# Layer 2 of a retention and two-layer feed-forward kernel: products of a folded pair accumulate in PSUM onto terms that ScalarE or VectorE wrote there, and a 256-token block keeps two tiles in a bank

## The chip, the cores and the metric

One core of a Trainium2 chip. The metric is device time in microseconds (us). A profile is one execution; engines are named as in it: PE (TensorE matmul), PEld (its weight loads), DVE (VectorE), ACT (ScalarE), POOL (GpSimd), SP (SyncE, which issues DMAs here).

## The reference

A retention (attention with a decay instead of a softmax) feeds two feed-forward layers over 2304 tokens:

```python
def _moe_ref(x, w_in, w_out):        # layer 1
    h = x @ w_in                     # 512 -> 2048
    g = np.maximum(0.01 * h, h)
    return g @ w_out                 # 2048 -> 512

def _moe2_ref(x, w_in, w_out):       # layer 2
    h = x @ w_in
    g = h - np.tanh(h)
    return g @ w_out

# reference: attn -> x (2304 x 512) -> layer 1 -> layer 2, all float32
```

## The kernel before

Every float32 operand of a feed-forward product is split into a high part (rounded) and a low part (the rest), and three matmuls stand for one: high x high, high x low, low x high.

The work of both layers is one list of steps. A step (m, g, t0, n, f) is one 128-wide tile of the hidden size in group g (four tiles, f = 0 to 3, are a group; there are four groups in a layer) for a block of n tokens from t0. The 2304 tokens are four blocks of 512 and one of 256. In layer 2 (m = 1) the block of 256 comes first in groups 0 to 2 and last in group 3. Let e be the first step of a layer-2 group: then e to e+3 are the 256-token steps and e+4 onward the 512-token steps.

What happens to a step s:

- `h_mm` or `h_folded` (PE) makes h, a 128 x n tile in one of three PSUM banks.
- `act_a` (ACT, then POOL): a square (L364), a tanh (L365), a second square (L372) and a Relu (L375), each reading what stands above it; POOL forms tanh times square (L368, called the cube below).
- `chain`: three DVE operations (h minus tanh, L387; a polynomial, L388; a predicated copy, L391), then ACT rounds the result into the high part of g (L393, the g copy) and POOL subtracts it for the low part (L394). The predicated copy is the last reader of the PSUM bank, which is then free.
- `o_mm` (PE): g times w_out, three steps later (`lag`), accumulated over a group in a second set of five banks: 12 matmuls of 512 columns for 512 tokens, 6 for 256 tokens; it can be issued in two halves (`part` 0 and 1).
- `evac` of the fourth step of a group moves or adds the sums to SBUF: in group 0 by copies that alternate between DVE (L497) and ACT (L495), later by DVE additions (L499).

In layer 2 a 512-token block is computed for two steps at a time (a *pair*, s and s+1): `h_folded` is a 2 x 2 block product with seven products in place of eight. Each product is 6 matmuls of 256 columns. It uses sums of weights (`ws`, prepared earlier) and differences of x (`xe`, made by `fold_x` between the last steps of layer 1 and the first pairs of layer 2: seven forms a block, each an ACT copy, L461, a POOL subtraction, L462, and for four of the seven a DVE subtraction, L459, ahead of them). The halves of the two banks p0 (for s) and p1 (for s+1) receive:

```python
        def first():
            product(a, left, of_x(0, 0), p1[:, left], start=True)
            product(sb, right, of_x(0, 1), p1[:, right])
            nc.scalar.activation(out=t_, in_=p1, func=AF.Copy)       # L318, 512 columns to SBUF
        def first_rest():
            product(a, right, of_x(1, 0), p0[:, left], start=True)
            product(sa, right, of_x(1, 1), p0[:, right], stop=True)
```

followed by four DVE additions of 256 columns (`add`, L303) that form the shared sums: p0 left, a sum in the tile mk, p0 right, and p1 right. The PE's order in a pair is: first (12 matmuls), half of the output product of step a = s-3, first_rest (12), its other half, second (6), half of step b = s-2, third (6), its other half, fourth (6).

The order of instructions on each engine is the order in which the Python code issues them, pair by pair and step by step (`layers`); each engine takes its own instructions in that order, with semaphores between engines. DMAs of weights and of stored xe tiles stand on SP's queue and are attached to steps (`splits`), as the forms of `fold_x` are.

Of the kernel before, what the change touches and what calls it, by code (L numbers as in the profile page):

```python
# [10 lines left out]
F32 = mybir.dt.float32  # L11
# [3 lines left out]
AF = mybir.ActivationFunctionType  # L15
ALU = mybir.AluOpType
PSUM = bass.MemoryType.PSUM

P = 128
# [4 lines left out]
LEAD = 16  # L24
# [11 lines left out]
def retention_moe_moe(  # L36
# [16 lines left out]
    nc = tc.nc  # L53
# [3 lines left out]
    KK = DM // P  # L57
# [5 lines left out]
    GF = 4  # L63
# [6 lines left out]
    pools = {}  # L70
# [56 lines left out]
    n_early = EARLY * GF  # L127

    def lag(s):
        return 2 if steps[s][0] == 0 else 3  # L130


    wide = w1i.dtype == I64
# [134 lines left out]
    def h_mm(s):  # L268
        m, g, t0, n, f = steps[s]
        w = wt[m, 0, g * GF + f]  # L270
        ps = pools["h"](s)
        for kk in range(KK):
            cs = slice(kk * P, (kk + 1) * P)
            for i, (wi, x) in enumerate(((0, xh), (0, xl), (1, xh))):
                nc.tensor.matmul(  # L275
                    out=ps[:, :n], lhsT=w[:, wi, cs], rhs=x[:, kk, t0:t0 + n],
                    start=kk == 0 and i == 0, stop=kk == KK - 1 and i == 2,
                )
        hp[s] = ps

    def h_folded(s):

        m, g, t0, n, f = steps[s]
        fg = g * GF + f
        a, b = wt[m, 0, fg], wt[m, 0, fg + 1]
        sa, sb = ws[fg][0], ws[fg][1]
        left, right = slice(0, HALF), slice(HALF, 2 * HALF)
        p0, p1 = pools["h"](s), pools["h"](s + 1)
        hp[s], hp[s + 1] = p0, p1

        def of_x(k, part):
            at = t0 + part * HALF
            return lambda i, kk: (xh, xl)[i][:, 2 * k + kk, at:at + HALF]

        def of_e(j):
            return lambda i, kk: xe[t0][:, j, i, kk, :]

        t_ = pools["t2"].tile([P, 512], F32, tag="t", name="t")
        mk = pools["t2"].tile([P, 512], F32, tag="mk", name="mk")
        early_tiles[s + 1] = t_, mk  # L300

        def add(out_, x, y):
            nc.vector.tensor_tensor(out=out_, in0=x, in1=y, op=ALU.add)  # L303

        def product(w, cols, x, out_, start=False, stop=False):
            for kk in range(2):
                at = cols.start + kk * P
                for j, (wi_, xi) in enumerate(((0, 0), (0, 1), (1, 0))):
                    nc.tensor.matmul(  # L309
                        out=out_, lhsT=w[:, wi_, at:at + P], rhs=x(xi, kk),  # L310
                        start=start and kk == 0 and j == 0, stop=stop and kk == 1 and j == 2,
                        skip_group_check=True,
                    )

        def first():
            product(a, left, of_x(0, 0), p1[:, left], start=True)
            product(sb, right, of_x(0, 1), p1[:, right])
            nc.scalar.activation(out=t_, in_=p1, func=AF.Copy)  # L318

        def first_rest():  # L320
            product(a, right, of_x(1, 0), p0[:, left], start=True)
            product(sa, right, of_x(1, 1), p0[:, right], stop=True)

        def first_sum():
            add(p0[:, left], p0[:, left], t_[:, left])

        def second():
            product(sa, left, of_e(0), p1[:, left])
            add(mk[:, left], p1[:, left], t_[:, right])

        def second_sum():
            add(p0[:, right], p0[:, right], mk[:, left])

        def third():
            product(sb, left, of_e(1), p1[:, left])
            add(p1[:, right], p1[:, left], t_[:, right])

        def fourth():
            product(b, right, of_e(2), p1[:, left], stop=True)

        return first, first_rest, first_sum, second, second_sum, third, fourth

    def g_at(s):
        m, g, t0, n, f = steps[s]
        at = LEAD if m == 0 and n < 512 else 0
        return slice(at, at + n)

    def act_a(s, tight=False):
        m, g, t0, n, f = steps[s]
        W, tp = pools["w"], pools["t"]  # L350
        h = hp[s][:, :n]
        if m == 0:
            gt = g_place(m)
            nc.scalar.activation(out=gt[:, 0, g_at(s)], in_=h, func=AF.Prelu, alpha=0.01)  # L354
            nc.scalar.activation(out=h, in_=h, func=AF.Prelu, alpha=0.01)
            tmp[s] = gt
            return
        u = tp.tile([P, W], F32, tag="u", name="u", bufs=3)
        v = u if tight else tp.tile([P, W], F32, tag="u", name="v", bufs=3)
        q = pools["t2"].tile([P, W], F32, tag="q", name="q", bufs=1)  # L360
# [14 lines left out]
        nc.scalar.activation(out=mk[:, :n], in_=u[:, :n], func=AF.Relu, bias=qb[:, 1:2])  # L375
        if tight:
            cube()
        tmp[s] = (v, t_, q, mk)

    def chain(s):  # L380
        m, g, t0, n, f = steps[s]
        h = hp.pop(s)[:, :n]
        if m == 0:
            v, gt = h, tmp.pop(s)
        else:
            v, t_, q, mk = (x[:, :n] for x in tmp.pop(s))
            nc.vector.tensor_tensor(out=h, in0=h, in1=t_, op=ALU.subtract)  # L387
            nc.vector.scalar_tensor_tensor(  # L388
                out=v, in0=q, scalar=RHO_A, in1=v, op0=ALU.add, op1=ALU.mult
            )  # L390
            nc.vector.copy_predicated(out=v, mask=mk.bitcast(U32), data=h)  # L391
            gt = g_place(m)
            nc.scalar.activation(out=gt[:, 0, g_at(s)], in_=v, func=AF.Copy)  # L393
        (nc.gpsimd if m else nc.vector).tensor_tensor(  # L394
            out=gt[:, 1, g_at(s)], in0=v, in1=gt[:, 0, g_at(s)].bitcast(F32), op=ALU.subtract
        )
        ga[s] = gt

    def o_mm(s, part=None):
        m, g, t0, n, f = steps[s]  # L400
# [11 lines left out]
        for d in {None: range(cnt), 0: range(cnt // 2), 1: range(cnt // 2, cnt)}[part]:  # L412
# [3 lines left out]
            for i, (wi, gi) in enumerate(((0, 0), (0, 1), (1, 0))):  # L416
                if m == 0:
                    l, r = w[:, wi, ds], gt[:, gi, g_at(s)]
                else:
                    l, r = gt[:, gi, ds], w[:, wi, :]  # L420

                nc.tensor.matmul(  # L422
                    out=o, lhsT=l, rhs=r,
                    start=f == 0 and i == 0 and d % pack == 0,
                    stop=f == GF - 1 and i == 2 and (d + 1) % pack == 0,
                    skip_group_check=pack > 1,
                )
# [450 lines left out]
    def layers():  # L878
        with ExitStack() as mc:
# [2 lines left out]
            cw_pool[0] = narrow.enter_context(  # L882
                tc.tile_pool(name="c1", bufs=2 * GF + 4, side="right")
            )
            ps_h = mc.enter_context(tc.tile_pool(name="ps_h1", bufs=3, space=PSUM))
            pools["h"] = lambda s: ps_h.tile([P, 512], F32, tag="h", name="h")
            pools["a"] = mc.enter_context(tc.tile_pool(name="ps_a1", bufs=5, space=PSUM))
            pools["w"] = 512

# [61 lines left out]
            e = per_group[1, 0][0]  # L951
            for t0, at in (
                (0, (-12, -11, -10, -9, -6, -6, -5)), (512, (-5, -5, -4, -4, -3, -3, -2)),
                (1024, (-2, -1, -1, 0, 4, 5, 6)), (1536, (7, 8, 9, 10, 12, 13, 14)),
            ):
                for i, op in zip(at, fold_x(t0)):
                    splits.setdefault(e + i, []).append(op)
# [23 lines left out]
            while s < end:  # L981
                m, g, t0, n, f = steps[s]
                if not folded(m, t0, n):
# [16 lines left out]
                first, first_rest, first_sum, second, second_sum, third, fourth = h_folded(s)  # L1000
                a, b = done[0], done[0] + 1
                assert (a, b) == (s - 3, s - 2)
                done[0] += 2
                first()
                o_mm(a, 0)
                first_rest()
                chain(s - 1)
                first_sum()
                cnt = steps[a][3] // P
                for d in range(cnt // 2):  # L1010
                    evac(a, d)
                o_mm(a, 1)
                evac(a, cnt // 2)
                second()
                second_sum()
                evac(a, cnt // 2 + 1)
                act_a(s)
                o_mm(b, 0)
                third()
                for op in splits.get(s, ()):  # L1020
                    op()
                o_mm(b, 1)
                fourth()
                act_a(s + 1)
                chain(s)
                assert steps[b][4] != GF - 1
# [79 lines left out]
```

## Time and profile before

| | us |
|---|---|
| median of 3 runs | 869.7 (869.04 to 871.87) |
| the profiled execution | 869.06, of it the span 867.1 |
| PE busy | 849.6 (98%) |
| DVE, ACT, POOL busy | 599.1 (69%), 452.0 (52%), 378.4 (44%) |
| layer 2 in the span | from about 474 to the end |

The page gives busy times over the whole span. Because PE is busy almost throughout, the views that matter are those by stretch: the chain of waits in order of time, which shows where it leaves PE, and the timelines of ACT, DVE and POOL around those places. A steady pair of layer 2 (24 matmuls of 512 columns and 42 of 256) follows the next without a gap.

### The profile page before, as it was taken

Reading aid. Unit: us, or ns where it says so; the run is one execution under the profiler, and the core shown is the slowest. Engines: PE = TensorE matmul, PEld = TensorE weight load, DVE = VectorE, ACT = ScalarE, POOL = GpSimd, SP = SyncE. Lnnn points to the kernel's source line nnn. Section 1 sums busy time; section 2 is a strip of 40 time slices with the busy share of each in tenths; the row PEclk is TensorE's granted clock in tenths of the full one; section 3 lists DMA queues with packets and bytes.
Section 4 is the critical chain, followed back from the end, with each engine's and each line's share of the span. In section 5 each row is a group of like instructions: output and inputs, shape, how many; then the busy total and the mean of one; then the engine's idle time right before and its main releaser. Section 6 shows DMA issues by size and latency. Waiting matters only on the chain.

```text
span 867.1 us, 15237 instructions
## 1 busy us (share of the span) xinstructions
PE 849.6 (98%) x5728; PEld 747.3 (86%) x5728; DVE 599.1 (69%) x1038; ACT 452.0 (52%) x899; POOL 378.4 (44%) x304
## 2 busy tenths in 40 slices
PE   6999999999999999999999999999999999999997
PEld 5889999888888888888888888888999899999996
DVE  5995777587786676658764677756666666666665
ACT  4553444453255334453544577666556566566663
POOL 2542222040036202464365587654555445545553
PEclk9999999999999999999999999999999999999999
DMA  9835663433464543644454512571225412563112
GB/s 341 315 122 173 219 208 122 146 121 113 134 211 189 179 121 99 243 170 136 181 184 156 195 73 74 222 285 73 78 96 183 159 73 74 207 231 122 49 50 74
DMA packets 38778, 134.43 MB, mean 155 GB/s; under 512 B 4400, under 2 KB 5936, under 8 KB 36656
## 3 DMA queue, kind: packets, MB, share of 16 engines
q1 hardware_dynamic: 38272, 133.25, 43.6%
q8 instruction: 45, 0.74, 0.3%
q10 hardware_dynamic: 432, 0.20, 0.1%
q14 instruction: 29, 0.24, 0.1%
HBM read 97.26 MB, written 36.18 MB: 154 GB/s over the span
## 4 chain that ended last, share of the span: by engine, by line
PE 90%; DVE 5%; issue 2%; POOL 2%; ACT 1%; DMA 0%; POOLq 0%; SPq 0%; DVEq 0%; ACTq 0%
PE a L422 39%; PE h L275 22%; PE h L309 17%; PE a L777 3%; PE x_b L752 3%; PE sc L626 2%; PE o L702 1%; PE o L691 1%; DVE cw L183 1%; DVE v L388 1%; PE x_c L659 1%; PE x_e L632 1%; POOL v L368 1%; DVE pt L640 1%; DMA qk<-in_kT 0%
## 5 line engine op out<-in xcount | busy, mean ns | idle before, releaser
L422 PE MATMUL a<-w 128*128 128x512 f32 (+1 forms) x1680 | 395.5, 377 | 1.2 <-ACT acc L495 0.6
L422 PEld LDWEIGHTS a<-w 128*128 128x128 f32 x1680 | 293.0, 188 | 49.9 <-POOL w L394 1.3
L256 POOL TENSOR_TENSOR w<-cw,w 128x512 fp32r<-128x512 f32 x80 | 112.7, 1427 | 234.1 <-ACT w L255 208.4
L275 PE MATMUL h<-xh,w 128*128 128x512 f32 (+1 forms) x672 | 187.1, 349 | 0.0
L368 POOL TENSOR_TENSOR v<-t,u 128x512 f32<-128x512 f32 (+1 forms) x76 | 93.8, 1234 | 113.7 <-ACT t L365 110.8
L275 PEld LDWEIGHTS h<-xh,w 128*128 128x128 f32 x672 | 119.5, 188 | 17.0
L354 ACT ACTIVATE w<-h 128x512 fp32r<-128x512 f32 (+1 forms) x68 | 37.2, 547 | 159.7 <-PE h L275 115.6
L394 POOL TENSOR_TENSOR w<-v,w 128x512 fp32r<-128x512 f32 (+1 forms) x76 | 97.1, 1277 | 47.8 <-ACT w L393 47.8
L275 PE MATMUL h<-xl,w 128*128 128x512 f32 (+1 forms) x336 | 117.0, 348 | 0.0
L309 PE MATMUL h<-xh,w 128*128 128x256 f32 x512 | 101.0, 281 | 0.4 <-DVE v L391 0.2
L364 ACT ACTIVATE u<-h 128x512 f32<-128x512 f32 (+1 forms) x80 | 44.3, 554 | 94.7 <-DVE h L303 67.6
L309 PEld LDWEIGHTS h<-xe,w 128*128 128x128 f32 x576 | 80.8, 189 | 10.6 <-DVE mk L303 2.6
L183 DVE SCALAR_TENSOR_TENSOR cw<-st,cw 128x512 uint32<-128x512 uint32 x96 | 86.5, 901 | 2.5
L388 DVE SCALAR_TENSOR_TENSOR v<-q,v 128x512 f32<-128x512 f32 (+1 forms) x76 | 55.7, 733 | 45.2 <-POOL v L368 45.0
L309 PEld LDWEIGHTS h<-xh,w 128*128 128x128 f32 x512 | 83.1, 190 | 3.3 <-DVE v L391 2.1
L309 PE MATMUL h<-xe,w 128*128 128x256 f32 x576 | 84.2, 282 | 1.2 <-DVE mk L303 1.2
L499 DVE TENSOR_TENSOR acc<-a,acc 128x512 f32<-128x512 f32 (+1 forms) x114 | 70.3, 656 | 16.2 <-PE a L422 16.2
L172 DVE TENSOR_SCALAR cw<-cw 128x512 f32<-128x512 f32 x64 | 33.9, 529 | 57.9 <-ACT cw L166 57.7
L309 PE MATMUL h<-xl,w 128*128 128x256 f32 x256 | 71.8, 281 | 0.0
L275 PEld LDWEIGHTS h<-xl,w 128*128 128x128 f32 x336 | 63.3, 188 | 8.6
L393 ACT ACTIVATE w<-v 128x512 fp32r<-128x512 f32 (+1 forms) x76 | 45.3, 596 | 46.9 <-DVE v L391 44.4
L387 DVE TENSOR_TENSOR h<-h,t 128x512 f32<-128x512 f32 (+1 forms) x80 | 51.4, 642 | 14.2 <-ACT t L365 13.2
(82 smaller groups left out, 1157.9 us busy)
## 6 DMA issues: line engine op xcount, KB each, us to landing
kept<-w SPq DMA_DIRECT2D x48, 512.0 KB, 3.4
w<-kept SPq DMA_DIRECT2D x48, 512.0 KB, 4.8
xe<-xkept SPq DMA_DIRECT2D x12, 1536.0 KB, 6.7
st<-in_w2i SPq DMA_DIRECT2D x16, 512.0 KB, 3.7
st<-in_w1i SPq DMA_DIRECT2D x12, 512.0 KB, 4.5
st<-in_w1o SPq DMA_DIRECT2D x12, 512.0 KB, 3.4
xkept<-xe SPq DMA_DIRECT2D x4, 1536.0 KB, 6.8
kv<-in_vn SPq DMA_DIRECT2D x16, 320.0 KB, 5.0
```

What stands on the lines that cost most here:

```text
L183: nc.vector.scalar_tensor_tensor(out=t["w"], in0=t[src], scalar=scalar, in1=t["w"], op0=op, op1=ALU.bitwise_or)
L256: nc.gpsimd.tensor_tensor(out=wp[:, 1, :], in0=wf, in1=wp[:, 0, :].bitcast(F32), op=ALU.subtract)
L275: nc.tensor.matmul(out=ps[:, :n], lhsT=w[:, wi, cs], rhs=x[:, kk, t0:t0 + n], start=kk == 0 and i == 0, stop=kk == KK - 1 and i == 2,)
L309: nc.tensor.matmul(out=out_, lhsT=w[:, wi_, at:at + P], rhs=x(xi, kk), start=start and kk == 0 and j == 0, stop=stop and kk == 1 and j == ...
L364: nc.scalar.activation(out=u[:, :n], in_=h, func=AF.Square)
L368: nc.gpsimd.tensor_tensor(out=v[:, :n], in0=t_[:, :n], in1=u[:, :n], op=ALU.mult)
L387: nc.vector.tensor_tensor(out=h, in0=h, in1=t_, op=ALU.subtract)
L388: nc.vector.scalar_tensor_tensor(out=v, in0=q, scalar=RHO_A, in1=v, op0=ALU.add, op1=ALU.mult)
L393: nc.scalar.activation(out=gt[:, 0, g_at(s)], in_=v, func=AF.Copy)
L394: (nc.gpsimd if m else nc.vector).tensor_tensor(out=gt[:, 1, g_at(s)], in0=v, in1=gt[:, 0, g_at(s)].bitcast(F32), op=ALU.subtract)
L422: nc.tensor.matmul(out=o, lhsT=l, rhs=r, start=f == 0 and i == 0 and d % pack == 0, stop=f == GF - 1 and i == 2 and (d + 1) % pack == 0, s ...
L499: nc.vector.tensor_tensor(out=dst, in0=a, in1=dst, op=ALU.add)
```

## The change

In a pair, ACT copies the left half of p1 into the left half of p0 (PSUM to PSUM), and the right half of p1 into t_ (SBUF), two copies of 256 columns for one of 512. The product that `first_rest` put into p0 with a start is now issued in `second`, without a start, on top of ACT's copy. The two sums that remain on DVE write p0 right and p1 right straight from p1 left and t_; the products `third_rest` and `fourth` come on top. PE's new order in a pair: first (12), half of a (6), second (12), the other half of a (6), third (6), third_rest (6), half of b (6), fourth (6), the other half of b (6). The number of matmuls is the same.

In the 256-token blocks of groups 0 to 2, two steps share a bank (`paired`): `act_a` and `chain` do nothing for the even step and run once, 512 columns wide, for the odd one. The output product of the first step of layer 2 is issued one step later (`lag` 4), inside the first pair. The PSUM banks of h are handed out from a list of free ones. The forms of `fold_x` for the two last blocks move: none is left in the first pair.

```diff
+    def paired(s):
+        return steps[s][0] == 1 and steps[s][3] == HALF and s < len(steps) - GF
+
+    h_free, h_bank = [0, 1, 2], {}
+
+    def h_tile(s, last=False):
+        h_bank[s] = h_free.pop(-1 if last else 0)
+        return pools["h"].tile([P, 512], F32, tag=f"h{h_bank[s]}", name="h")
...
-        p0, p1 = pools["h"](s), pools["h"](s + 1)
+        p0, p1 = h_tile(s, last=True), h_tile(s + 1)
...
         def first():
             product(a, left, of_x(0, 0), p1[:, left], start=True)
             product(sb, right, of_x(0, 1), p1[:, right])
-            nc.scalar.activation(out=t_, in_=p1, func=AF.Copy)
-
-        def first_rest():
-            product(a, right, of_x(1, 0), p0[:, left], start=True)
-            product(sa, right, of_x(1, 1), p0[:, right], stop=True)
-
-        def first_sum():
-            add(p0[:, left], p0[:, left], t_[:, left])
+            nc.scalar.activation(out=p0[:, left], in_=p1[:, left], func=AF.Copy)
+            nc.scalar.activation(out=t_[:, left], in_=p1[:, right], func=AF.Copy)
 
         def second():
+            product(a, right, of_x(1, 0), p0[:, left])
             product(sa, left, of_e(0), p1[:, left])
-            add(mk[:, left], p1[:, left], t_[:, right])
+
+        def add(out_):
+            nc.vector.tensor_tensor(out=out_, in0=p1[:, left], in1=t_[:, left], op=ALU.add)
 
         def second_sum():
-            add(p0[:, right], p0[:, right], mk[:, left])
+            add(p0[:, right])
 
         def third():
             product(sb, left, of_e(1), p1[:, left])
-            add(p1[:, right], p1[:, left], t_[:, right])
+            add(p1[:, right])
+
+        def third_rest():
+            product(sa, right, of_x(1, 1), p0[:, right], stop=True)
...
     def act_a(s, tight=False):
         m, g, t0, n, f = steps[s]
         W, tp = pools["w"], pools["t"]
+        if paired(s):
+            if f % 2 == 0:
+                return
+            n = 512
...
-                (1024, (-2, -1, -1, 0, 4, 5, 6)), (1536, (7, 8, 9, 10, 12, 13, 14)),
+                (1024, (-2, -2, -1, -1, 6, 7, 8)), (1536, (9, 9, 10, 11, 12, 13, 14)),
...
+                first()
+                while done[0] < s - 3:
+                    o_mm(done[0])
+                    evac(done[0])
+                    done[0] += 1
                 a, b = done[0], done[0] + 1
                 done[0] += 2
-                first()
                 o_mm(a, 0)
-                first_rest()
+                second()
                 chain(s - 1)
-                first_sum()
                 cnt = steps[a][3] // P
                 for d in range(cnt // 2):
                     evac(a, d)
+                second_sum()
                 o_mm(a, 1)
-                evac(a, cnt // 2)
-                second()
-                second_sum()
-                evac(a, cnt // 2 + 1)
+                third()
+                for d in range(cnt // 2, cnt):
+                    evac(a, d)
+                third_rest()
                 act_a(s)
                 o_mm(b, 0)
-                third()
                 for op in splits.get(s, ()):
                     op()
+                fourth()
                 o_mm(b, 1)
-                fourth()
                 act_a(s + 1)
                 chain(s)
```

## Rows read from the trace of the kernel before

**Rows 1.** Busy by stretch: start:end, length; PE, PEld, DVE, ACT, POOL; clock; DMA
```profile
500.00:510.00 10.00, 8.78 (x57) 7.65 (x55) 7.57 (x13) 7.66 (x14) 8.30 (x7) 1.00 0.15 61
...
486.57:569.30 82.73, 80.59 (x513) 71.53 (x512) 60.62 (x95) 57.35 (x105) 57.38 (x42) 1.00 0.31 121
569.30:664.00 94.70, 94.69 (x603) 85.50 (x602) 61.25 (x109) 58.05 (x110) 48.74 (x40) 1.00 0.36 134
664.00:841.77 177.77, 177.68 (x1131) 160.96 (x1130) 118.71 (x207) 107.22 (x196) 91.87 (x72) 1.00 0.35 128
841.77:867.10 25.33, 20.02 (x108) 16.41 (x107) 14.20 (x23) 10.59 (x26) 9.80 (x11) 0.97 0.18 63
```

**Rows 2.** Chain of waits in order of time, layer 2: start, length, engine, tile, line
```profile
486.57 1.41 PE h L309 x12
...
569.30 1.41 PE h L275 x12
...
664.00 1.41 PE h L275 x12
...
726.81 2.12 PE h L309 x18
728.93 1.36 PE a L422 x6
...
737.19 2.12 PE h L309 x18
...
841.77 1.41 PE h L275 x12
```

**Rows 3.** Waits of PE after 470: who for whom, total, times, longest
```profile
PE h L309 <- DVE mk L303: 1.2, 1, 1.2
```

**Rows 4.** Timeline of ACT: group 1's 256-token steps and first pairs, a steady pair
```profile
574.06 0.37 ACT L364 ACTIVATE u<-h 128x256 f32<-128x256 f32 x1
...
590.39 0.60 ACT L364 ACTIVATE u<-h 128x512 f32<-128x512 f32 x1 [3.50 <-DVE h L303]
...
594.92 0.61 ACT L393 ACTIVATE w<-v 128x512 fp32r<-128x512 f32 x1
595.44 0.58 ACT L318 ACTIVATE t<-h 128x512 f32<-128x512 f32 x1
...
727.60 0.60 ACT L364 ACTIVATE u<-h 128x512 f32<-128x512 f32 x1 [0.87 <-POOL v L368]
```

**Rows 5.** Timeline of PE: group 0's start, a late start, group 1, a steady pair
```profile
485.03 1.54 PE L422 MATMUL a<-w 128*128 128x512 f32 x6
...
502.69 0.97 PE L309 MATMUL h<-xe,w 128*128 128x256 f32 x6 [1.22 <-DVE mk L303]
...
594.48 0.38 PE L309 MATMUL h<-xh,w 128*128 128x256 f32 x1
...
726.64 0.87 PE L309 MATMUL h<-xe,w 128*128 128x256 f32 x6
```

**Rows 6.** Timeline of ACT in group 0: square to copy, with forms of fold_x between
```profile
503.22 0.60 ACT L364 ACTIVATE u<-h 128x512 f32<-128x512 f32 x1 [0.67 <-DVE h L303]
...
505.42 0.63 ACT L461 ACTIVATE xe<-acc 128x512 fp32r<-128x512 f32 x1
...
508.65 0.63 ACT L461 ACTIVATE xh<-acc 128x512 fp32r<-128x512 f32 x1
509.17 0.60 ACT L318 ACTIVATE t<-h 128x512 f32<-128x512 f32 x1
```

**Rows 7.** Timeline of DVE: step e+1 of group 0; a chain in group 1
```profile
483.01 0.42 DVE L387 TENSOR_TENSOR h<-h,t 128x256 f32<-128x256 f32 x1
...
595.14 0.69 DVE L388 SCALAR_TENSOR_TENSOR v<-q,v 128x512 f32<-128x512 f32 x1
595.94 0.74 DVE L391 COPY_PREDICATED v<-mk,h 128x512 f32<-128x512 uint32 x1
```

**Rows 8.** Timeline of POOL: the low part of g in group 1
```profile
595.61 1.38 POOL L394 TENSOR_TENSOR w<-v,w 128x512 fp32r<-128x512 f32 x1 [0.50 <-ACT w L393]
```

More of the change, by code (lines that the diff above doesn't have):

```diff
@@ L129, in lag @@
     def lag(s):
-        return 2 if steps[s][0] == 0 else 3
+        if steps[s][0] == 0:
+            return 2
+        return 4 if s == per_group[1, 0][0] else 3
+    def paired(s):
[4 more added lines that the diff above has]
+        return pools["h"].tile([P, 512], F32, tag=f"h{h_bank[s]}", name="h")
     wide = w1i.dtype == I64
@@ L270, in h_mm @@
         w = wt[m, 0, g * GF + f]
-        ps = pools["h"](s)
+        two = paired(s)
+        half = two and f % 2
+        ps = hp.pop(s - 1) if half else h_tile(s + two)
+        at = half * n
         for kk in range(KK):
@@ L275, in h_mm @@
                 nc.tensor.matmul(
-                    out=ps[:, :n], lhsT=w[:, wi, cs], rhs=x[:, kk, t0:t0 + n],
-                    start=kk == 0 and i == 0, stop=kk == KK - 1 and i == 2,
+                    out=ps[:, at:at + n], lhsT=w[:, wi, cs], rhs=x[:, kk, t0:t0 + n],
+                    start=not half and kk == 0 and i == 0,
+                    stop=(half or not two) and kk == KK - 1 and i == 2,
+                    skip_group_check=two,
                 )
@@ L298, in h_folded @@
         t_ = pools["t2"].tile([P, 512], F32, tag="t", name="t")
[L299 to L303, printed above, removed]
+        early_tiles[s + 1] = t_, pools["t2"].tile([P, 512], F32, tag="mk", name="mk")
         def product(w, cols, x, out_, start=False, stop=False):
@@ L317, in first, with g_cols @@
             product(sb, right, of_x(0, 1), p1[:, right])
-            nc.scalar.activation(out=t_, in_=p1, func=AF.Copy)
-        def first_rest():
-            product(a, right, of_x(1, 0), p0[:, left], start=True)
-            product(sa, right, of_x(1, 1), p0[:, right], stop=True)
-        def first_sum():
-            add(p0[:, left], p0[:, left], t_[:, left])
+            nc.scalar.activation(out=p0[:, left], in_=p1[:, left], func=AF.Copy)
+            nc.scalar.activation(out=t_[:, left], in_=p1[:, right], func=AF.Copy)
         def second():
+            product(a, right, of_x(1, 0), p0[:, left])
             product(sa, left, of_e(0), p1[:, left])
-            add(mk[:, left], p1[:, left], t_[:, right])
+        def add(out_):
+            nc.vector.tensor_tensor(out=out_, in0=p1[:, left], in1=t_[:, left], op=ALU.add)
         def second_sum():
-            add(p0[:, right], p0[:, right], mk[:, left])
+            add(p0[:, right])
         def third():
             product(sb, left, of_e(1), p1[:, left])
-            add(p1[:, right], p1[:, left], t_[:, right])
+            add(p1[:, right])
+        def third_rest():
+            product(sa, right, of_x(1, 1), p0[:, right], stop=True)
         def fourth():
             product(b, right, of_e(2), p1[:, left], stop=True)
-        return first, first_rest, first_sum, second, second_sum, third, fourth
+        return first, second, second_sum, third, third_rest, fourth
     def g_at(s):
         m, g, t0, n, f = steps[s]
-        at = LEAD if m == 0 and n < 512 else 0
+        at = LEAD if m == 0 and n < 512 else f % 2 * n if paired(s) else 0
         return slice(at, at + n)
+    def g_cols(s):
+        return slice(0, 512) if paired(s) else g_at(s)
     def act_a(s, tight=False):
@@ L381, in chain @@
         m, g, t0, n, f = steps[s]
+        if paired(s):
+            if f % 2 == 0:
+                return
+            n = 512
         h = hp.pop(s)[:, :n]
+        h_free.append(h_bank.pop(s))
         if m == 0:
@@ L392, in chain @@
             gt = g_place(m)
-            nc.scalar.activation(out=gt[:, 0, g_at(s)], in_=v, func=AF.Copy)
+            nc.scalar.activation(out=gt[:, 0, g_cols(s)], in_=v, func=AF.Copy)
         (nc.gpsimd if m else nc.vector).tensor_tensor(
-            out=gt[:, 1, g_at(s)], in0=v, in1=gt[:, 0, g_at(s)].bitcast(F32), op=ALU.subtract
+            out=gt[:, 1, g_cols(s)], in0=v, in1=gt[:, 0, g_cols(s)].bitcast(F32),
+            op=ALU.subtract,
         )
         ga[s] = gt
+        if paired(s):
+            ga[s - 1] = gt
     def o_mm(s, part=None):
@@ L419, in o_mm @@
                 else:
-                    l, r = gt[:, gi, ds], w[:, wi, :]
+                    c = g_at(s).start + d * P
+                    l, r = gt[:, gi, c:c + P], w[:, wi, :]
                 nc.tensor.matmul(
@@ L884, in layers @@
             )
-            ps_h = mc.enter_context(tc.tile_pool(name="ps_h1", bufs=3, space=PSUM))
-            pools["h"] = lambda s: ps_h.tile([P, 512], F32, tag="h", name="h")
+            ps_h = mc.enter_context(tc.tile_pool(name="ps_h1", bufs=1, space=PSUM))
+            pools["h"] = ps_h
             pools["a"] = mc.enter_context(tc.tile_pool(name="ps_a1", bufs=5, space=PSUM))
@@ L999, in layers @@
                     continue
-                first, first_rest, first_sum, second, second_sum, third, fourth = h_folded(s)
+                first, second, second_sum, third, third_rest, fourth = h_folded(s)
+                first()
[3 more added lines that the diff above has]
+                    done[0] += 1
                 a, b = done[0], done[0] + 1
```

## The prediction, made before the changed kernel was run

> **What bounds the kernel now.** I read the busy times by stretch first, then the chain of waits in order of time over layer 2, then the timelines of ACT, DVE and POOL at the places where the chain leaves PE.
>
> The stretches [rows 1] show PE busy for 177.68 of 177.77 us in groups 2 and 3, and 94.69 of 94.70 in group 1; DVE, ACT and POOL are busy for two thirds or less of these. The chain [rows 2] gives the price of a matmul in a full stream: 18 of 256 columns in 2.12 us, 0.1178 each, and six of 512 in 1.36, 0.2267 each. A pair has 42 and 24 of them, 10.38, and this is the distance of 726.81 from 737.19: a steady pair has nothing to give. What an edit can save is only what PE loses against this count:
> - group 0, 486.57 to 569.30: 82.73. It holds eight pairs (336 narrow matmuls, 39.6) and 174 wide ones (39.4): 79.0, lost 3.7.
> - group 1, to 664.00: 94.70. 384 narrow, 216 wide: 94.2, lost 0.5.
> - groups 2 and 3, to 841.77: 177.77. 720 narrow, 408 wide: 177.3, lost 0.5.
>
> So 4.7 us in all. The tail after 841.77 keeps its code (the last group's 256-token block is not paired). The losses lie where pairs follow a 256-token block, whose output products are half as long; the largest single wait is for a DVE sum into mk [rows 3], a sum that goes.
>
> **Part by part.** *Matmuls:* same number, same sizes: 0.
>
> *DVE sums, two of four gone:* in a steady pair DVE is not on the chain: 0. In group 0 and after 256-token blocks the waits for them go with the 4.7, which I count as returned in full; what comes in their place is priced next.
>
> *ACT's copy comes onto PE's path.* This decides. Before, ACT's copy into t_ (L318) was read by DVE only, and PE needed p1 left free for second, after 12 more matmuls and half an output product. Now second begins by accumulating onto the copy in p0, so PE stops after first and half of a until it has landed, and the rest of PE's queue (second, a's other half, third and on) stands behind it. On ACT the copy stands behind everything issued before it: four operations of act_a(s), four of act_a(s+1), the g copy of s. These start when third_rest of the pair ahead has ended. I compare two times from that end to second.
>
> PE's side, steady: half of b (1.36), fourth (0.71), other half of b (1.36), first (1.41), half of a (1.36): 6.20. In the second pair after a 256-token block, b and a are 256-token steps: three halves of 0.68, so 4.16.
>
> ACT's side: 0.25 from the end of the last slot to the square (fourth's six matmuls from 726.64 end their slots at 727.35 [rows 5], the square starts at 727.60 [rows 4]); square to copy with ACT never idle 5.05 (590.39 to 595.44 [rows 4], just this place in group 1); the copy; 0.10 to restart PE (six matmuls that had waited took 0.97, otherwise 0.87 [rows 5]). A 256-column copy from PSUM to PSUM is not in the trace: below, half of the copy of 512 columns, 0.29; above, that copy itself, 0.58; the nearest row, a 256-column square out of PSUM, is 0.37 [rows 4], and I take it. Sum 5.77. The Trainium skill ("ScalarE: Activation LUTs", section "What ACT_TABLE_LOAD costs") puts an ACTIVATE with immediate operands at 186 ns plus 0.833 ns a column, by estimate 0.40 here; by it the seven waits counted below would be 0.2 longer together.
>
> - Steady pairs: 6.20 against 5.77, room of 0.43: 0. A copy of 0.58 still fits.
> - Second pair after the block, groups 0, 1 and 2: 5.77 - 4.16 = 1.6 each, 4.8 in all. Before, first_rest was issued there at 594.48 [rows 5] while the copy began at 595.44 [rows 4], and nobody waited for it.
> - Pairs of group 0 with forms of fold_x. Each form puts an ACT copy into that run: 503.22 to 509.17 with two of them is 5.95 [rows 6], so 6.67 against 6.20, wait 0.5; a third adds 0.52 (508.65 to 509.17), wait 1.0; one alone fits. By the new positions the runs that end in the third, fifth and sixth pair have two, that of the fourth three: 3 x 0.5 + 1.0 = 2.5. In the three, the odd step's form waits besides for its DVE subtraction, which is queued behind the predicated copy: from 0 to about 1 us each, I take 0.2, so 0.6. Together 3.1; bounds 0 (if ACT catches up) and 5.5.
>
> *The 256-token block, two tiles a bank.* Fewer, wider operations (0.60 for 512 columns against 2 x 0.37 on ACT [rows 4]) on engines with room: 0 for groups 1 and 2. But the pair's g comes later than the first tile's alone did. In group 0 DVE starts this chain at 483.01, held by four evacuations [rows 7]; subtract (0.6 to the next), polynomial (0.8 to the next), predicated copy 0.74 [rows 7], g copy 0.61 [rows 4], POOL 1.38 [rows 8], with 0.05 to 0.1 between engines: low part ready at about 487.3. PE reaches the product of step e, moved behind first, at 485.03 + 1.41 = 486.44 [rows 5], and needs the low part at its second matmul, 486.67: wait 0.7 (0 to 1.0). In groups 1 and 2 this product has two steps more, no wait.
>
> *First and second pairs:* the copy and the first DVE sum are each covered by half a product of 0.68 only, and need about 0.7: 0.05 each time, 0.15 a group, 0.45 in all.
>
> *Banks:* first now writes the bank that was free longest, so it waits for no predicated copy; ACT's copy into the other comes later than that bank's last reader. 0 (the saving is in the 4.7). *Forms moved ahead of layer 2:* one step of layer 1 gets one more; PE has not lost there: 0, up to 0.5.
>
> Sum: 0.7 + 4.8 + 3.1 + 0.45 = 9.05 lost against 4.7 lost now: +4.3. The profiled execution took 869.06 (span 867.1 and about 2 around it): 873.4. The median shown is 0.64 above that execution, so 874.0 as a median.
>
> **Rivals.**
> 1. *Faster: DVE was the limit and ACT keeps time.* For it: PE's largest wait is for DVE. Place: second in the second pair of groups 0 to 2. It decides from where ACT's run from square to copy is under 3.4 us (4.16 less 0.25, 0.37 and 0.10). Then the waits for copies are gone in every pair, the 4.7 come back less 1.15 for the product of e and the short covers: 869.06 - 3.6 + 0.64 = 866.1. Against it: the 5.05 is the same nine operations at the same place, measured.
> 2. *No change: only the short second pairs wait.* If forms find room (ACT's run begins earlier, or DVE without two sums lets them through), losses are 0.7 + 4.8 + 0.45 = 5.95 against 4.7: 871.0. For it: two forms miss the cover by 0.5 only. Against it: DVE does not order these ACT copies.
> 3. *Steady pairs wait too.* The room of 0.43 goes where the copy is as long as one of 512 columns (0.2 more) and a predicated copy holds the g copy by 0.3 or more: 0.1 to 0.3 in each of some 20 pairs, 4 on top: 878.
> 4. *The clock falls.* PE now stands still 1.6 us at a time. The longest stand in the trace is 1.2 us, and the stretch around it has a granted clock of 1.00, the 2.4 GHz level [rows 1]; the tail, with more idling, 0.97. At 1.2 GHz the 10.38 of a pair could double, +10 after each of three such waits: 900. The Trainium skill ("TensorE: Matmul & The Clock Gate", section "HAM oscillation — how this bites in real kernels") warns of this level where PE idles between bursts; no run here yet shows it.
>
> That the change does not do what it says is not a case of its own: the code leaves no other order on ACT.
>
> **How the numbers follow.** A measurement of this kernel can tell about 0.3%, 2.6 us, from no change: same is 867.1 to 872.3. Forecast 0.66, own range 871 to 877 (forms from 0 to 5.5, the product of e from 0 to 1): of it 0.54 slower, 0.12 same. Rival 1, 0.10: 0.08 faster, 0.02 same (it could return half). Rival 2, 0.13: same. Rival 3, 0.09: slower. Rival 4, 0.02: slower. That gives faster 0.08, same 0.27, slower 0.65. Range 870.0 to 878.0: it leaves out rival 1, rival 4 and half of rival 3.
>
> **What would show it.** In the chain of waits, PE after half of a in the second pair of groups 0, 1 and 2 released by an ACT copy into h, idle 1.6 us; the same, 0.5 to 1.0 us, in the third to sixth pair of group 0; the second matmul of step e released by POOL's low part. No wait for a DVE sum over 0.2. Groups 1 and 2 each about 1.2 us longer than now, the pairs after their second 10.38 apart. The prediction is wrong if the ACT copies end before PE has issued half of a in these pairs, or if steady pairs are not 10.38.

## The result and the profile after

The changed kernel takes 874.49 us (median of 6 runs, 873.78 to 876.14), the kernel before 870.05 (6 runs, 869.04 to 871.87): a ratio of 1.0052, 95% interval 1.0037 to 1.0067. It is slower, by half a per cent; 874.0 was forecast. The profiled execution took 874.01, its span is 872.2.

First the page's busy times of the changed kernel, then its busy times by stretch (columns as in [rows 1]). The stretches begin at the first step of groups 0, 1 and 2 of layer 2 and at the last group's 256-token block:

```profile
PE 850.6 (98%) x5728; PEld 746.7 (86%) x5728; DVE 570.3 (65%) x956; ACT 451.7 (52%) x901; POOL 370.9 (43%) x292
```
```profile
473.99:571.53 97.54, 93.76 (x590) 82.40 (x590) 58.40 (x84) 62.50 (x119) 60.83 (x45) 1.00 0.37 137
571.53:667.69 96.16, 94.78 (x603) 85.34 (x602) 54.22 (x86) 58.03 (x108) 46.85 (x36) 1.00 0.36 132
667.69:846.99 179.30, 177.90 (x1130) 160.91 (x1130) 105.30 (x168) 107.73 (x202) 88.43 (x68) 1.00 0.35 126
846.99:872.20 25.21, 20.02 (x108) 16.41 (x107) 13.93 (x22) 9.44 (x24) 9.63 (x11) 0.94 0.18 63
```

DVE does 28.8 us less in all, and the kernel is longer. Groups 1, and 2 with 3, now take 96.16 and 179.30, before 94.70 and 177.77 [rows 1]: 1.5 more each. Group 0 takes 97.54; before it went from 474.05, the first row below, to 569.30 [rows 2], 95.25: 2.3 more. The tail is what it was. These make 5.3, and the spans differ by 5.1.

```profile
474.05 1.41 PE h L275 x12
```

What PE waited for in layer 2, first as the matmuls have it and then as the weight loads have it (total, times, longest):

```profile
PE h L321 <- DVE v L412: 4.2, 3, 1.4
PE h L321 <- ACT h L330: 1.7, 4, 0.8
PE a L450 <- POOL w L418: 0.9, 3, 0.4
PE h L321 <- DVE h L338: 0.3, 1, 0.3
```
```profile
PEld h L321 <- ACT h L330: 9.6, 11, 1.8
PEld h L321 <- DVE h L338: 2.9, 8, 0.7
```

L330 is the copy into p0, L338 a DVE sum, L418 the low part of g. The three longest waits stand under DVE's polynomial (L412), which PE does not read. The timelines around the second pair of group 1 show what happened, ACT first, then DVE, PE and PE's weight loads:

```profile
592.59 0.60 ACT L383 ACTIVATE u<-h 128x512 f32<-128x512 f32 x1 [2.38 <-PE h L321]
...
597.11 0.61 ACT L417 ACTIVATE w<-v 128x512 fp32r<-128x512 f32 x1
597.63 0.36 ACT L330 ACTIVATE h<-h 128x256 f32<-128x256 f32 x1
597.93 0.36 ACT L331 ACTIVATE t<-h 128x256 f32<-128x256 f32 x1
```
```profile
597.34 0.69 DVE L412 SCALAR_TENSOR_TENSOR v<-q,v 128x512 f32<-128x512 f32 x1
```
```profile
595.83 0.84 PE L450 MATMUL a<-w 128*128 128x512 f32 x3
598.04 0.38 PE L321 MATMUL h<-xh,w 128*128 128x256 f32 x1 [1.38 <-DVE v L412]
```
```profile
598.04 0.19 PEld L321 LDWEIGHTS h<-xh,w 128*128 128x128 f32 x1 [1.80 <-ACT h L330]
```

PE has issued half of a at 596.51 (595.83 and three of 0.2267) and starts second at 598.04: 1.53 later, 0.05 after ACT's copy ended. The polynomial ended at 598.03, 0.04 after the copy. The profile infers the releaser from semaphore events, and for the matmul it named the later of the two, for the weight load the copy; e2 below shows that it is the copy. ACT's run from square to copy is 5.04 (592.59 to 597.63), before 5.05 at this place [rows 4]: the same run, which PE did not have to await then.

A steady pair has room, as forecast. ACT's copy, PE's second and the second of the next pair, in group 3:

```profile
776.10 0.36 ACT L330 ACTIVATE h<-h 128x256 f32<-128x256 f32 x1
```
```profile
776.89 0.28 PE L321 MATMUL h<-xh,w 128*128 128x256 f32 x1
...
787.28 0.28 PE L321 MATMUL h<-xh,w 128*128 128x256 f32 x1
```

The copy ends 0.43 before PE would go on in any case, and the pairs there keep their distance of 10.38 (10.39 by these two rounded times).

### The profile page after: what moved, and what is told of

Its sections match the earlier page's. It is cut to its first block, busy times and chain, and to the rows that moved or that the text cites. A ratio compares the mean times of both kernels' runs of the same rounds, so it can differ in the third digit from the quotient of the medians.

```text
span 872.2 us, 15121 instructions
## 1 busy us (share of the span) xinstructions
PE 850.6 (98%) x5728; PEld 746.7 (86%) x5728; DVE 570.3 (65%) x956; ACT 451.7 (52%) x901; POOL 370.9 (43%) x292
## 4 chain that ended last, share of the span: by engine, by line
PE 87%; DVE 4%; ACT 3%; DMA 2%; POOL 2%; issue 2%; POOLq 0%; ACTq 0%; SPq 0%; DVEq 0%
PE a L450 38%; PE h L289 21%; PE h L321 17%; PE a L805 3%; PE x_b L780 3%; PE o L730 1%; PE sc L654 1%; PE o L719 1%; DVE cw L194 1%; DMA cm_sb<-in_cmask 1%; POOL v L387 1%; DMA acc<-in_w1i 1%; ACT q L391 1%; DVE pt L668 1%; DVE v L412 1%
## 5 line engine op out<-in xcount | busy, mean ns | idle before, releaser
L387 POOL TENSOR_TENSOR v<-t,u 128x512 f32<-128x512 f32 x70 | 92.2, 1317 | 130.2 <-ACT t L384 124.7
L289 PEld LDWEIGHTS h<-xh,w 128*128 128x128 f32 x672 | 119.5, 188 | 17.1
L321 PE MATMUL h<-xh,w 128*128 128x256 f32 x512 | 106.7, 282 | 5.9 <-DVE v L412 4.2
L418 POOL TENSOR_TENSOR w<-v,w 128x512 fp32r<-128x512 f32 x70 | 91.1, 1301 | 45.5 <-ACT w L417 45.5
L321 PEld LDWEIGHTS h<-xh,w 128*128 128x128 f32 x512 | 85.4, 190 | 11.6 <-ACT h L330 9.6
L527 DVE TENSOR_TENSOR acc<-a,acc 128x512 f32<-128x512 f32 (+1 forms) x114 | 70.7, 656 | 22.2 <-PE a L450 22.2
L321 PEld LDWEIGHTS h<-xe,w 128*128 128x128 f32 x576 | 78.4, 189 | 7.4 <-DVE h L338 2.9
L412 DVE SCALAR_TENSOR_TENSOR v<-q,v 128x512 f32<-128x512 f32 x70 | 53.8, 768 | 33.2 <-POOL v L387 31.5
L338 DVE TENSOR_TENSOR h<-h,t 128x256 f32<-128x256 f32 x64 | 27.7, 432 | 63.6 <-PE h L321 62.3
```

Source lines behind the costliest of these rows:

```text
L289: nc.tensor.matmul(out=ps[:, at:at + n], lhsT=w[:, wi, cs], rhs=x[:, kk, t0:t0 + n], start=not half and kk == 0 and i == 0, stop=(half or ...
L321: nc.tensor.matmul(out=out_, lhsT=w[:, wi_, at:at + P], rhs=x(xi, kk), start=start and kk == 0 and j == 0, stop=stop and kk == 1 and j == ...
L412: nc.vector.scalar_tensor_tensor(out=v, in0=q, scalar=RHO_A, in1=v, op0=ALU.add, op1=ALU.mult)
L418: (nc.gpsimd if m else nc.vector).tensor_tensor(out=gt[:, 1, g_cols(s)], in0=v, in1=gt[:, 0, g_cols(s)].bitcast(F32), op=ALU.subtract,)
L527: nc.vector.tensor_tensor(out=dst, in0=a, in1=dst, op=ALU.add)
```

## Experiments

Eleven variants were run beside the kernel before. The part of the span ahead of layer 2 differs by up to 2.4 us between profiles though its code hardly does, so I compare stretches of layer 2, from the first step of one group to that of the next, in us. The ratios hold that part as well: e2 is 3.2 us above the changed kernel by the ratios and 1.8 by the stretches.

| kernel | group 0 | group 1 | groups 2, 3 | ratio to before (95%) |
|---|---|---|---|---|
| before | 95.25 | 94.70 | 177.77 | |
| changed | 97.54 | 96.16 | 179.30 | 1.0052 (1.0037 to 1.0067) |
| e1_no_copy | 96.67 | 95.67 | 178.75 | 1.0036 (1.0023 to 1.0049) |
| e2_wide_copy | 98.51 | 96.56 | 179.76 | 1.0089 (1.0074 to 1.0104) |
| e3_block_only | 94.47 | 94.70 | 177.75 | 0.9988 (0.9979 to 0.9997) |
| e4_body_only | 99.28 | 96.17 | 179.24 | 1.0071 (1.0057 to 1.0085) |
| e5_dve_copy | 101.11 | 99.53 | 182.20 | 1.0168 (1.0149 to 1.0187) |
| e6_forms_only | 93.77 | 94.68 | 177.78 | 0.9984 (0.9975 to 0.9993) |
| e7_no_act | 96.53 | 95.60 | 178.74 | 1.0028 (1.0018 to 1.0039) |
| e8_evac_first | 93.78 | 94.67 | 177.80 | 0.9987 (0.9978 to 0.9996) |
| e9_no_act_no_sum | 92.64 | 94.61 | 177.70 | 0.9952 (0.9939 to 0.9966) |
| e10_evac_act | 92.30 | 94.66 | 177.78 | 0.9968 (0.9958 to 0.9979) |
| e11_no_sum | 96.62 | 95.88 | 178.93 | 1.0042 (1.0025 to 1.0058) |

**Is it ACT's copy? Take it away (e1), make it wider (e2).**

```diff
# e1
-            nc.scalar.activation(out=p0[:, left], in_=p1[:, left], func=AF.Copy)
-            product(a, right, of_x(1, 0), p0[:, left])
+            product(a, right, of_x(1, 0), p0[:, left], start=True)
# e2
-            nc.scalar.activation(out=p0[:, left], in_=p1[:, left], func=AF.Copy)
+            nc.scalar.activation(out=p0, in_=p1, func=AF.Copy)
```

> The changed kernel without ACT's copy of p1 left into p0 left; the term that the copy carries is left out of the result, and the product that came on top of it starts its bank itself. Theory (PE waits for this copy, which stands in ACT's queue behind nine operations of the pair ahead): the waits in the second pair of groups 0 to 2 (1.5 each) and in pairs three to six of group 0 (0.5, 1.0, 0.5, 0.5) go, with about 0.1 of restart each: 867 (0.997 of before). What is left in the second pairs is a wait for the predicated copy that frees p0's bank, 0.1 to 0.2. Rival (the wait in the second pairs is for DVE's polynomial, as the trace's releaser column has it, and ACT's copy only ends about then): those three waits stay, 871.

> The changed kernel with ACT's first copy of a pair made 512 columns wide (all of p1 into all of p0); the right half of p0 is written over by DVE's sum later. Theory: the copy takes about 0.58 instead of 0.36, so each of the seven waits for it grows by 0.22 and the run of one form (pair seven of group 0) begins to wait by 0.2: +1.7, 876.2 (1.007 of before); steady pairs, with room of 0.43, stay at 10.38. Rival (PE waits for something else that ends about then): 874.5, no change. Rival (steady pairs have no room): some 20 pairs by 0.2, +4 more, 880.

e2 did as the theory says: layer 2's three stretches grew by 1.8 against the changed kernel (1.7 expected), steady pairs did not, but for 0.2 in one of group 2. Its waits of PE name the copy in all places, seven of them, as many as had been counted:

```profile
PE h L321 <- ACT h L330: 7.4, 7, 1.6
```

With the copy's end moved by 0.2, the polynomial no longer coincides with it. But e1 missed: 1.9 came back of 5.3, not some 7. PE's waits in e1:

```profile
PE h L321 <- DVE h L337: 1.5, 4, 0.8
PE h L321 <- ACT t L330: 1.0, 3, 0.3
```

L330 is here ACT's other copy, which reads p1 right; PE waits for it before it writes p1 left. L337 is DVE's first sum. So the copy into p0 does hold PE, but something stands right behind it.

**What stands behind it (e7, e9, e11).** e7 leaves out both copies, e11 the first DVE sum, e9 all three.

```diff
# e7, against e1
-            nc.scalar.activation(out=t_[:, left], in_=p1[:, right], func=AF.Copy)
-            nc.vector.tensor_tensor(out=out_, in0=p1[:, left], in1=t_[:, left], op=ALU.add)
+            nc.vector.tensor_tensor(out=out_, in0=p1[:, left], in1=xl[:, 0, :HALF].bitcast(F32), op=ALU.add)
# e9, against e7
         def second_sum():
-            add(p0[:, right])
+            pass
# e11, against the changed kernel
         def second_sum():
-            add(p0[:, right])
+            pass
-            product(sa, right, of_x(1, 1), p0[:, right], stop=True)
+            product(sa, right, of_x(1, 1), p0[:, right], start=True, stop=True)
```

> The changed kernel with neither of ACT's copies in a pair: the term that the first carries is left out (the product on top of it starts its bank itself), and DVE's sums take another SBUF operand of the same size in place of t_. Theory, revised after the run without the first copy alone (PE waits for ACT's queue, and the other copy, which also reads p1, stands in the same place of it): now nothing of second waits for ACT; group 0 takes about 93.5, group 1 95.4 and groups 2 and 3 178.5, together as before: 1.000. What is left is a wait of 0.3 for the predicated copy that frees p0's bank, and waits for DVE's sums behind the chain. Rival (the second pair is short of everything, and the waits pass to DVE and the banks): little change against the run without one copy, 1.003 or more.

> The kernel without ACT's two copies, and without DVE's first sum as well (p0 right from p1 left); the terms of the copy and of this sum are left out. The third product and third_rest then wait for neither engine. Theory (two waits lie one behind the other on PE's new order: ACT's copy ahead of second, and DVE's first sum, queued behind the chain of the step before, ahead of third; each hides the other): group 0 92.7, group 1 94.6, groups 2 and 3 177.8 from first step to first step, 0.994 of before with the rest as it is; left are the product of step e (0.55) and the predicated copies that free p0's bank. Rival (the second pairs are held by the banks or by POOL): as without the copies alone, 96.5, 95.6 and 178.7, 1.003.

> The changed kernel with both of ACT's copies but without DVE's first sum of a pair (p0 right from p1 left; left out of the result, and third_rest starts its half itself). It completes the four cases: both waits 1.0052 of before, no copies 1.0028, neither 0.9952. Theory (the two waits lie one behind the other on PE, and the first, for ACT, is the longer; the sum's wait shows only where ACT's is gone): the seven waits for ACT's copy stay, only what PE waits for the sum in the changed kernel goes (0.5 in pair six of group 0, some 0.1 in each first and second pair): 1.004 of before, group 0 96.6, groups 1 and 2 95.9 and 179.0. Rival (the two add): what the sum cost without the copies, 0.0076, goes here too: 0.9976.

e7 went to its rival: 96.53, 95.60 and 178.74. Its waits of PE, and where one of them ends, on DVE and on PE in the second pair of group 1:

```profile
PE h L321 <- DVE h L336: 3.8, 7, 0.9
PE a L448 <- POOL w L416: 0.9, 3, 0.4
PE h L321 <- DVE v L413: 0.5, 3, 0.2
```
```profile
597.14 0.74 DVE L413 COPY_PREDICATED v<-mk,h 128x512 f32<-128x512 uint32 x1
597.78 0.67 DVE L525 TENSOR_TENSOR acc<-a,acc 128x512 f32<-128x512 f32 x1
598.37 0.42 DVE L336 TENSOR_TENSOR h<-h,xl 128x256 f32<-128x256 f32 x1
```
```profile
598.85 0.95 PE L321 MATMUL h<-xe,w 128*128 128x256 f32 x6 [0.64 <-DVE h L336]
```

second ends sooner, and then third waits for the sum, which is queued behind the chain of the step before and an evacuation. In the changed kernel this wait hid behind ACT's. The four cases settle it, and the last two came out within 0.1 us of the numbers written beforehand in each stretch:

| | with the sum | without |
|---|---|---|
| with the copies | 1.0052 | 1.0042 |
| without | 1.0028 | 0.9952 |

Taking away the sum alone is worth 0.0010, the copies alone 0.0024, both 0.0100. The first of these is within the noise of the ratios; by the three stretches the gains are 1.6, 2.1 and 8.1 us. Two waits stand one behind the other on PE, each covered by half an output product only.

**Which part of the change costs, and which gains (e3, e4, e6).** e3 has the old pair and the rest of the change; e4 the new pair without the rest; e6 is the kernel before with the moved forms alone.

```diff
# e4, against the changed kernel
     def paired(s):
-        return steps[s][0] == 1 and steps[s][3] == HALF and s < len(steps) - GF
+        return False
# e6, against the kernel before
-                (1024, (-2, -1, -1, 0, 4, 5, 6)), (1536, (7, 8, 9, 10, 12, 13, 14)),
+                (1024, (-2, -2, -1, -1, 6, 7, 8)), (1536, (9, 9, 10, 11, 12, 13, 14)),
```

(e4 also has `lag` and the forms of the kernel before; e3's edit is `h_folded` and the pair of `layers` put back.)

> The pair as it was before (one copy of 512 columns to SBUF, four DVE sums, first_rest and second in the old order), with the other parts of the change: two tiles a bank in 256-token blocks, banks from a list, the later product of step e, moved forms. Theory (the price is the copy alone, the block part is about even): group 0 loses 3 to 3.5 (0.55 at the product of e, 0.5 in pair two, the rest with forms), groups 1 and 2 0.5 each: 869 to 870, 0.998 to 1.000 of before. Rival (the later g of two tiles a bank costs in groups 1 and 2): those 1.5 longer each, 872 or more.

> Only the pair's new order and copies (and banks from a list): 256-token blocks with a bank and a chain for each step, forms and the product of e where they were before. Theory: groups 1 and 2 lose 2.0 each as in the changed kernel (1.5 in the second pair); group 0 has no wait at the product of e, but two forms in the first pair's run: 2.6 in pair two, 0.5 in pairs three, four and six; in all 873.9 (1.0045 of before). Rival (two tiles a bank cause the long second pair): groups 1 and 2 back to 0.5 each, 871.

> The kernel before with one line of the change: the later positions of the forms of fold_x for the two last blocks (none left in the first pair of layer 2, one more on each of the two steps ahead of it). Theory (what the block part gained, 0.8 us, came from the forms that left the first two pairs): group 0 from 95.25 to about 93.8 from its first step to that of group 1, groups 1 and 2 as before; 0.998 of before. Rival (the gain was that of two tiles a bank): no gain, 1.000.

e3 is faster than before by 0.12%: the new pair costs 6.1 us (373.00 less 366.92 over the three stretches). e4 has the changed kernel's groups 1 to 3 to 0.1 us, so two tiles a bank are not what makes the second pairs long. Its group 0 was 1.7 longer than the changed kernel's, where about 0.6 less was expected (873.9 against 874.5). The two forms left in the first pair stand in the run that ends in pair two: PE stood there for 2.46 (497.43 to 499.89), about as expected. What was not expected is a wait of 0.9 for the copy in the first pair (ahead of 489.51), and the clock. PE around the second pair, then its stretch with the granted clock (third number from the end):

```profile
496.75 0.84 PE L450 MATMUL a<-w 128*128 128x512 f32 x3
499.89 0.58 PE L321 MATMUL h<-xh,w 128*128 128x256 f32 x1 [2.31 <-ACT h L330]
...
503.63 0.87 PE L321 MATMUL h<-xe,w 128*128 128x256 f32 x6
```
```profile
499.80:502.90 3.10, 3.00 (x13) 3.01 (x14) 2.80 (x3) 0.97 (x3) 2.65 (x3) 0.51 0.00 0
```

After that stand the granted clock was 0.51, the 1.2 GHz level. The 12 narrow and three wide matmuls from 499.89 took 3.74 in place of 2.09, of which 0.1 is the restart: the lower clock cost about 1.5.

e6 shows that the gain of e3 is that of the forms, 1.5 us, and that two tiles a bank with the later product of step e (and banks from a list) give back 0.7 of it (94.47 against 93.77).

In e4 a 256-token tile is alone in its bank. The Trainium skill ("PSUM — Partial Sum Buffer", section "The four PSUM rules") says that writes of VectorE and ScalarE do not mark an element as written, so a product without a start replaces them where the bank was cleared and PE has not written since; by it the products of third_rest after such a block replace DVE's sum in e4. No trace shows this.

**Another queue for the copy (e5).**

```diff
-            nc.scalar.activation(out=p0[:, left], in_=p1[:, left], func=AF.Copy)
+            nc.vector.tensor_copy(out=p0[:, left], in_=p1[:, left])
...
                 second()
-                chain(s - 1)
-                for d in range(cnt // 2):
-                    evac(a, d)
                 second_sum()
+                chain(s - 1)
...
                 third()
-                for d in range(cnt // 2, cnt):
+                for d in range(cnt):
                     evac(a, d)
```

> The changed kernel with the copy of p1 left into p0 left on DVE in place of ACT, and DVE's first sum issued ahead of the chain of the step before (the evacuation of a after the second sum). Theory (which queue the copy stands in is the price): on DVE it stands behind the predicated copy, which ends 1.0 us before ACT's copy would begin; the second pair waits 0.55 for it and 0.3 for ACT's other copy, in place of 1.5; the pairs with forms hardly wait, 0.2 at most; later DVE chains cost up to 0.5 in each second pair: about 871, 1.001 of before. Rival (any copy there costs as much): 874, 1.005.

A clear miss, 1.7% slower. The large waits are in the first pair after each 256-token block: 2.9 in three for the g copy, and some 0.8 each, of the 3.5 in six, for the low part of g. In group 1:

```profile
599.08 0.50 PE L450 MATMUL a<-w 128*128 128x512 f32 x1 [0.98 <-ACT w L417]
600.43 1.22 PE L450 MATMUL a<-w 128*128 128x512 f32 x2 [0.85 <-POOL w L418]
```
```profile
601.00:604.00 3.00, 3.00 (x12) 2.66 (x11) 1.43 (x2) 1.20 (x4) 0.61 (x1) 0.54 0.00 0
```

Both follow the chain of the block's last two tiles. I had priced the copy and not what stands behind it on DVE: DVE stops before the sum until PE has ended second, and the chain and four evacuations come after. Every second steady pair loses 0.3 as well (182.20), for an output bank that the first of these evacuations frees late (DVE L527):

```profile
813.65 0.53 PEld L450 LDWEIGHTS a<-w 128*128 128x128 f32 x3 [0.44 <-DVE acc L527]
```

After the two stands of 1.1 each in group 1 the granted clock was 0.54 from 601 to 604 (the row above), the 1.2 GHz level, and 0.52 from 499.0 to 501.5 after the like in group 0; in group 2, after the same two, it stayed at 1.00. So part of this miss is the clock. As it changes two things at once, it does not say which queue is better.

**A version faster than both (e8, e10).** In group 0 of e6, PE still waits 0.8 for banks that ACT evacuates late (the first row below; the second is from e8).

```profile
PE a L422 <- ACT acc L495: 0.8, 2, 0.6
```
```profile
PE h L309 <- DVE mk L303: 0.8, 2, 0.6
```

```diff
# e10, against e6, group 0 of layer 2 only
-                if d % 2:
+                if d < 2 if m else d % 2:
...
                 first_rest()
...
+                early = steps[a][1] == 0
+                if early:
+                    for d in range(cnt // 2):
+                        evac(a, d)
                 chain(s - 1)
                 first_sum()
...
                 second_sum()
+                if early:
+                    evac(a, cnt // 2)
                 evac(a, cnt // 2 + 1)
```

> The kernel before with the moved forms, and in group 0 ACT's evacuation of the second row block of step a issued ahead of the g copy of the step before (a g copy waits for DVE's predicated copy, and PE's next output products wait for the bank that the evacuation frees: 0.8 us in two waits in the run of the block part alone). Theory: these waits go, group 0 1.0 shorter than with the moved forms alone: 0.997 of before. Rival (the bank that PE waits for is the fourth row block's, freed as late as before): as with the moved forms alone.

> The kernel before with the moved forms, and in group 0 of layer 2 ACT evacuates the first two row blocks of step a, ahead of the g copy of the step before, and DVE the last two, after the second sum. Theory (moving one ACT evacuation alone only passed PE's wait for a bank on to a wait for the DVE sum into mk, because a DVE evacuation still stood ahead of that sum): both waits go, group 0 92.9 in place of 93.8; 0.9975 of before. Rival (the chain with its slow polynomial, 1.77 beside POOL, holds the sum by itself): 93.8, 0.9985 as with the moved forms alone.

e8 (e6 with only the second row block's evacuation ahead of the chain) gained nothing: PE's wait for ACT's evacuation went, and one of 0.8 for the DVE sum into mk took its place. e10 takes DVE's evacuations out of that sum's way as well: PE is busy for 92.22 of the 92.30 us of group 0.

```profile
475.67:567.97 92.30, 92.22 (x590) 82.80 (x590) 66.91 (x105) 62.70 (x120) 62.59 (x49) 1.00 0.38 145
```

Its ratio, 0.9968 (0.9958 to 0.9979), is below that of the kernel before and of the changed one.

## Why the prediction was right

- *A full PE is the bound, and only lost time can be gained.* Right: steady pairs are 10.38 in both kernels, and 28.8 us less on DVE bought nothing.
- *ACT's side 5.77 against PE's 4.16 in second pairs, 1.6.* Measured 1.54 in group 0 (496.93, three slots after the first row below, to 498.47), 1.53 in group 1, and 0.10 for the restart behind each, which the 5.77 holds: 1.6. The copy, taken as 0.37, has a median of 0.365 over 32. The 0.40 by the Trainium skill ("ScalarE: Activation LUTs", section "What ACT_TABLE_LOAD costs") was 0.03 too long here, and the measurement decides.

```profile
496.25 0.84 PE L450 MATMUL a<-w 128*128 128x512 f32 x3
498.47 0.39 PE L321 MATMUL h<-xh,w 128*128 128x256 f32 x1 [1.38 <-DVE v L412]
```

- *Pairs of group 0 with forms: 0.5, 1.0, 0.5, 0.5, and 0.2 more in three.* Measured 0.47, 0.96, 0.49, 0.46, and 0.10 for each restart: 2.8 in all for 3.1. The 0.2 for the DVE subtraction ahead of the odd form were not there: ACT paused in none of the four runs. The longest:

```profile
515.68 0.63 ACT L489 ACTIVATE xe<-acc 128x512 fp32r<-128x512 f32 x1
516.20 0.59 ACT L383 ACTIVATE u<-h 128x512 f32<-128x512 f32 x1
...
518.39 0.65 ACT L417 ACTIVATE w<-v 128x512 fp32r<-128x512 f32 x1
518.91 1.16 ACT L489 ACTIVATE xh<-acc 128x512 fp32r<-128x512 f32 x2
519.95 0.39 ACT L330 ACTIVATE h<-h 128x256 f32<-128x256 f32 x1
```

- *Product of step e, 0.7.* Measured 0.55: the second matmul at 487.16, due 0.23 after the first at 486.38.

```profile
486.38 0.40 PE L450 MATMUL a<-w 128*128 128x512 f32 x1
487.16 2.12 PE L450 MATMUL a<-w 128*128 128x512 f32 x8 [0.38 <-POOL w L418]
```

- *DVE's sums: two fewer, the rest hidden.* Too simple, and the term that was short. In pair six of group 0, third waited 0.48 for the first sum (545.12, six slots after the first row below, to 545.60), against "No wait for a DVE sum over 0.2":

```profile
543.76 1.54 PE L450 MATMUL a<-w 128*128 128x512 f32 x6
545.60 0.96 PE L321 MATMUL h<-xe,w 128*128 128x256 f32 x6 [0.30 <-DVE h L338]
```

With the small waits of first and second pairs, the first sum cost 1.6 (what e11 gives back), where the forecast had 0.45 for the sum and the copy together. So group 0 lost 6.0 (5.55 forecast), groups 1 and 2 2.0 each (1.75): 10.0 in place of 9.05, which is the 5.3 against 4.3.

- *Rival 1, DVE was the limit and 4.7 come back.* Wrong as a forecast. But the prediction, too, took ACT's copy as the only thing on PE's path ("This decides"). By the three stretches e1 is still 3.4 us longer than the kernel before, and e7, without both of ACT's copies, 3.1, because the DVE sum takes the wait over. The forecast could do without this second wait, because in these places ACT's is the longer of the two and hides it.
- *Rivals 2 and 3.* Out: the pairs with forms did wait, 2.8 in all, and steady pairs stayed at 10.38.
- *Rival 4, the clock.* Out for the changed kernel: with waits of 1.5 us the granted clock stays at 1.00, the 2.4 GHz level, in all three stretches. So the section of the Trainium skill that the prediction cites ("TensorE: Matmul & The Clock Gate", section "HAM oscillation — how this bites in real kernels") brings no loss here. But the rival was nearer than its chance of 0.02 says: in e4, after one stand of 2.46, and in e5, after two of 1.1 close together, the clock did fall. The price given for it, 10 for each fall, was too high; the fall in e4 cost about 1.5. (The 1.2 that the prediction calls the longest stand of the trace is that of layer 2; ahead of it PE waits up to 5.3 for a DMA.)

That the total came so close is partly luck. By the stretches the change costs 5.3 and not 4.3: with their restarts the pairs with forms took 0.3 less than forecast, the second pairs 0.1 more and DVE's first sum 1.1 more. The medians happen to differ by 4.4.

## What to carry to other kernels

Where the busiest engine is full in the steady state, work taken from an idle engine buys nothing, but a new dependency can cost: before a product is put on top of what another engine writes, add up that engine's queue from its last release to the write, and compare it with what PE has to issue in between, in the shortest stage and not in the steady one. Taking the suspected wait away is only half a test; look at what stands behind it, and take both away. The gain lay elsewhere, in the order of ACT and DVE work at the transition, where 3 us of PE's lost time could be recovered with two small reorderings (e10). And look at the clock of a variant before its time is put down to the waits alone.

## What the runs showed of the hardware

The releaser of a wait can be a coincidence: the matmul row named DVE's polynomial in three waits, the row of the weight loads named the copy, and lengthening the copy by 0.2 made all seven matmul waits name it. PE also waits for ACT's read of one half of a PSUM bank before it writes the other half (e1, 1.0 in three waits); whether the chip or the order set by the semaphores asks for this was not tried. The granted clock stayed at 1.00 over stands of 1.5 us (the changed kernel), fell to the 1.2 GHz level after one of 2.46 (e4), and after two of 1.1 close together it fell in two places of three (e5).
